# Ending instruction-prefetch hints before the second phase, and a refitted instruction order, in a memory-augmented transformer block

## The chip, the cores and the metric

The kernel runs on one core of a Trainium2 chip, as one program. The metric is the device time of one execution in microseconds, as a median of runs. A core has five engines that run their own instruction streams side by side: TensorE (PE, matmuls; its weight loads are listed as PEld), VectorE (DVE), ScalarE (ACT), GpSimd (POOL) and SyncE (SP, which issues the DMAs here). They wait for each other through semaphores.

## What is computed

A sequence of 2048 tokens (512 wide, bf16) goes through a layer norm and an attention layer with 32 heads of 128, in 64 segments of 32 tokens. Each segment attends to itself and to 8 memory tokens, and the memory of the next segment is the attention's output for those 8 tokens. So the 64 segments are a chain. Then comes an MLP (512 to 1792 to 512, gelu) over all tokens, with residuals.

```python
for s in range(n_seg):                                  # 64
    xs = x[:, s * seg_len:(s + 1) * seg_len, :].copy()
    h = jnp.concatenate([mem, xs], axis=1)              # 8 + 32 rows
    q = jnp.einsum('btd,dhe->bhte', h, Wq)
    k = jnp.einsum('btd,dhe->bhte', h, Wk)
    v = jnp.einsum('btd,dhe->bhte', h, Wv)
    scores = jnp.einsum('bhqe,bhke->bhqk', q, k) * scale
    scores = jnp.where(mask[None, None], scores, -1000000000.0)
    p = _softmax(scores, axis=-1)
    o = jnp.einsum('bhqk,bhke->bhqe', p, v)
    o = jnp.einsum('bhte,hed->btd', o, Wo)
    mem = o[:, :M, :].copy()                            # 8 rows go on to s + 1
    outs.append(o[:, M:, :])
...
h = x + _A_ref(_layernorm(x, axis=-1), ...)
h2 = h + _B_ref(_layernorm(h, axis=-1), ...)            # gelu(y @ w1 + b1) @ w2 + b2
```

## The kernel before

**Two phases.** The first phase walks through the 64 segments. Four segments make a block of 128 tokens; a segment's place in its block (0 to 3) is called first to fourth segment here. The second phase is the MLP, in four groups of 512 tokens.

**A segment on PE.** 24 of its 32 tokens and the 8 memory tokens are one group of 32 rows (A); the remaining 8 tokens of four segments are packed into one group of 32 rows per block (B). The parts of a segment have names:

- K0, K1, Q0, Q1, V0, V1: the projections of A, half the heads each. One is four passes over the inner dimension (L680; L446 where the weights of the pass before are kept in place and not loaded again), each of four matmuls side by side.
- SC0, SC1: scores of the memory rows and of B (L821); PV0, PV1: their products with the values (L851, L855).
- SA: scores of the A rows (L880); PVA: their product with the values (L906), done in the segment after.
- WO: the output projection in eight units (L943). Its memory rows, turned by DVE (TT, L955) and added (hT, L949), are what K0 of the next segment waits for.
- F0, F1: projections of the next block's B rows, in the first three segments of a block; FB: the output projection of the B rows, in the fourth.
- TR: a layer norm or a residual step that brings no PE work in most segments.

Between them the other engines empty PSUM and do the softmax. On ACT: kqP0 to kqP3 (projections out of PSUM), EC (exp of SC), VS (values), OT (outputs), prefills of PSUM with masks ("ps"). On DVE: KA and QT (32x32 transposes of keys and queries), nmc, rsc, PC, PTC (softmax of SC), nma, SA, sma, rsa, PTA (softmax of SA), TT and hT, opA and opB, xr, st and st2 with ag and ag2 (layer norm statistics). On POOL: ZC (copies of queries that SC needs), PA (part of SA's softmax).

**What sets the order.** PE's order is written out by hand in ORDER, one row for each of a block's four segments, with slices of parts ("K0", 0, 3 is the first three passes of K0). BANKS gives the PSUM bank of each part, BACK says which projections run through the inner dimension backwards (so that weights can be kept). The other engines' orders come from a list scheduler, Sched.schedule, that works with assumed durations: each operation has a rank (the longest way to the end) plus a bonus by its kind, from the table BONUS, and is placed on its engine in the earliest gap. Where an operation may run on several engines (for example ZC on ACT, DVE or POOL), the earliest end wins, and DVE is charged LEAN on top. DMAs are issued by SP, in the order of their planned starts.

**Instruction pages and hints.** Sched.far cuts PE's stream so that a branch lies near the end of each stretch of 256 instructions. Cut k has a branch that is never taken (zero < 0) to the place two cuts further on, and a prefetch hint for it that stands just after the cut before. The branch's fall-through is the next instruction, so the program's order isn't changed by it. The hint names a target three pages ahead of the page that it stands in. At the last two cuts there is a plain branch to the next instruction and no hint. In the kernel before there are 173 cuts.

Of the kernel before, what the change touches and what calls it, by code (L numbers as in the profile page):

```python
# [19 lines left out]
OVERLAP = {"act": 0.1, "dve": 0.077, "pool": -0.06, "sp": 0.0}  # L20
DMA_SEMS = 100
STIR = 12
LINE_N, LINE_AT, LINE_HINT, LINE_LAST, LINE_FIRST, LINE_Q, LINE_W = 256, 192, 172, 228, 80, 24, 0.005
HALVES = ("kqP", "KA", "ZCm", "QA", "VS", "nmc", "EC", "rsc", "PC", "PTC", "OTm", "KB", "QTB", "VSB", "QT")
BONUS = {"EC1": -9.35, "KA1": -9.25, "KB0": 1.83, "KB1": 1.99, "OTB": -7.01, "OTm1": 2.33, "PA": 4.46, "PC0": -2.44, "PC1": -9.37,
         "PTA": -0.66, "PTC0": -17.49, "QT0": 16.34, "QT1": -16.16, "QTB0": -4.17, "SA": -3.48, "TT": 3.09, "VBD": 15.9, "VS0": -6.6,
         "VS1": -4.52, "VSB1": -1.12, "ZCb": -3.7, "ZCm0": 4.94, "ZCm1": 0.49, "ag": 40, "ag2": -18.63, "hTx": 5.11, "hd": 4.63,
         "kqP0": -1.58, "kqP1": -0.51, "kqP2": 0.34, "kqP3": 16.53, "kqP4": 8.98, "kqP5": -11.25, "nma": 2.14, "nmc0": 10.03, "nmc1": 7.47,
         "opA": -22.54, "opB": -40, "ps": -10.18, "rs": 9.93, "rs2": -4.63, "rsa": 3.13, "rsc0": 3.57, "rsc1": -3.63, "sma": -5.97,
         "st": 4.73, "st2": -7.47, "vd": -9.08, "xT": 3.91, "xn": 4.97, "xn4": 0.15, "xr": -40}  # L30
LEAN = 7.140

ORDER = (
          (("K0", 0, 4), ("Q0", 0, 4), ("Q1", 0, 4), ("K1", 0, 4), ("SC0", 0, 1), ("V0", 0, 1), ("TR", 0, 1), ("V0", 1, 4), ("V1", 0, 2),
           ("SC1", 0, 1), ("F0", 0, 2), ("V1", 2, 3), ("PVA", 0, 1), ("PV0", 0, 1), ("V1", 3, 4), ("F0", 2, 4), ("WO", 0, 2),
           ("PV1", 0, 1), ("WO", 2, 8), ("F1", 0, 4), ("SA", 0, 1)),
          (("K0", 0, 3), ("Q0", 0, 1), ("K0", 3, 4), ("Q0", 1, 4), ("Q1", 0, 4), ("K1", 0, 4), ("SC0", 0, 1), ("V0", 0, 1), ("TR", 0, 1),
           ("V0", 1, 4), ("V1", 0, 2), ("SC1", 0, 1), ("F0", 0, 1), ("V1", 2, 3), ("F0", 1, 2), ("PVA", 0, 1), ("PV0", 0, 1), ("V1", 3, 4),  # L40
           ("F0", 2, 4), ("WO", 0, 2), ("PV1", 0, 1), ("WO", 2, 8), ("F1", 0, 4), ("SA", 0, 1)),
          (("K0", 0, 4), ("Q0", 0, 4), ("Q1", 0, 4), ("K1", 0, 4), ("SC0", 0, 1), ("V0", 0, 1), ("TR", 0, 1), ("V0", 1, 4), ("V1", 0, 2),
           ("SC1", 0, 1), ("F0", 0, 1), ("V1", 2, 3), ("F0", 1, 2), ("PVA", 0, 1), ("PV0", 0, 1), ("V1", 3, 4), ("F0", 2, 4), ("WO", 0, 2),
           ("PV1", 0, 1), ("WO", 2, 8), ("F1", 0, 4), ("SA", 0, 1)),
          (("K0", 0, 3), ("Q0", 0, 1), ("K0", 3, 4), ("Q0", 1, 4), ("Q1", 0, 4), ("K1", 0, 4), ("SC0", 0, 1), ("PVA", 0, 1), ("V0", 0, 1),
           ("TR", 0, 1), ("V0", 1, 4), ("SC1", 0, 1), ("FB", 0, 1), ("V1", 0, 3), ("PV0", 0, 1), ("V1", 3, 4), ("FB", 1, 4), ("WO", 0, 2),
           ("PV1", 0, 1), ("WO", 2, 8), ("FB", 4, 8), ("SA", 0, 1)),
)
BANKS = (
    dict(Q0=5, Q1=7, K0=4, K1=5, V0=7, V1=5, SC0=6, SC1=4, F0=6, F1=5, FB=5, SA=7, WO=4),  # L50
    dict(Q0=5, Q1=7, K0=4, K1=5, V0=7, V1=5, SC0=6, SC1=4, F0=6, F1=5, FB=5, SA=7, WO=4),
    dict(Q0=5, Q1=7, K0=6, K1=5, V0=7, V1=5, SC0=6, SC1=4, F0=6, F1=5, FB=6, SA=7, WO=4),
    dict(Q0=5, Q1=7, K0=4, K1=5, V0=7, V1=5, SC0=6, SC1=4, F0=5, F1=7, FB=6, SA=7, WO=4),
)
BACK = (("Q0", "Q1", "V1"), ("Q0", "Q1", "V0", "F0", "F1"), ("Q1", "K0", "V0", "F0", "F1"), ("Q0", "V1"))
BANK0 = dict(K0=7, K1=5, Q0=6, Q1=7, V0=4, V1=5, SC0=4, SC1=6, F0=6, F1=4, FB=6, SA=4, WO=5)
START = (("B", "V", 0, (6, 7)), "V0", "V1", ("B", "K", 0, (4, 6)), "K0", "K1", ("B", "K", 1, (4, 6)), ("B", "V", 1, (7, 5)),
         ("B", "Q", 0, (4, None)), "Q0", ("B", "Q", 0, (None, 5)), "Q1", "Z", "SC0", "SC1", ("B", "Q", 1, (5, 7)), "PV0", "PV1", "SA", "WO")
# [24 lines left out]
class Sched:  # L83
# [89 lines left out]
    def schedule(self):  # L173
# [25 lines left out]
        def push(o):  # L199
            heapq.heappush(heap, (-o.rank - BONUS.get(o.kind, 0.0), o.gidx, o))  # L200
        for o in self.rec:
# [13 lines left out]
        for o in order:  # L215
# [13 lines left out]
            for eng, (fn, dur) in (o.alts or {o.eng: (o.fn, o.dur)}).items():  # L229
                L, ST = lines[eng], starts[eng]  # L230
                i = bisect.bisect_right(ST, t)
                while True:
# [7 lines left out]
                    i += 1  # L240
                cost = s + dur + (LEAN if eng == "dve" and o.alts else 0.0)
                if best is None or cost < best[0]:
# [77 lines left out]
    def far(self, nc, e, zero):  # L320

        ops = self.streams["pe"]
        early, per, m = None, [], 0
        for o in ops:
            per += [o.dur / o.ni] * o.ni
        n, lines, cuts, cand = 0, -2, [], []
        for i, o in enumerate(ops):
            line, at = divmod(n - LINE_AT, LINE_N)
            if early is None and line == -1 and at >= LINE_FIRST:
                early = i  # L330
                n += 1
                line, at = divmod(n - LINE_AT, LINE_N)
            if cand and (line > cand[0][0] or at >= LINE_LAST):
                cuts.append(max(cand, key=lambda c: c[1:])[-1])
                lines = cand[0][0]
                cand = []
                n += 2
                line, at = divmod(n - LINE_AT, LINE_N)
            if line > lines and at >= LINE_HINT:
                assert at < 240  # L340
                cand.append((line, min(sum(per[max(0, m - LINE_Q):m]), 0.4) + min(sum(per[m:m + LINE_Q]), 0.3) + at * LINE_W, i))
            m += o.ni
            n += o.ni + (len(o.waits) >= 2)
        cuts += [c[-1] for c in cand[-1:]]
        home, mark, k = nc.cur_bb.parent, None, 0
        for i, o in enumerate(ops):
            if i == early:
                mark = e.mark_branch_hint_location()
            if k < len(cuts) and cuts[k] == i:
                if k + 2 < len(cuts):  # L350
                    b = e.br_lt(zero, 0, on_true="line%d" % (k + 2), on_false="line%d" % k)
                    if mark is not None:
                        b.branch_hint(mark)
                    nc.switch_bb("line%d" % k, parent=home)
                    mark = e.mark_branch_hint_location()
                else:
                    e.br("line%d" % k)
                    nc.switch_bb("line%d" % k, parent=home)
                k += 1
            yield o  # L360
# [103 lines left out]
def build_kernel(nc, A_x, A_mem0, A_Wq, A_Wk, A_Wv, A_Wo, B_w1, B_b1, B_w2, B_b2, out):  # L464
# [3 lines left out]
    with st:  # L468
# [461 lines left out]
        def wo_units(lhs, reads, bank, idle=None):  # L930

            for q in range(8):
                if idle and q == 4:
                    stir(*idle)

                def f(e, q=q):
                    for k in (2 * q, 2 * q + 1):
                        for a in range(2):

                            h = (k // 8) * 16 + 8 * a + k % 8  # L940
                            for b in range(2):
                                j = 2 * a + b
                                ins = e.matmul(ps[bank][32 * j:32 * j + 32, 0:256], lhs(slot(h)), wo_cols(h, b), start=(k == 0), stop=(k == 15),  # L943
                                               tile_position=(0, 32 * j), skip_group_check=True)
                    return ins
                S.op("pe", f, reads=[("WO", 2 * (q // 4) + g) for g in range(2)] + reads(q // 4), writes=[("ps", bank)], dur=0.2185, mode=MC, ni=16)
# [4 lines left out]
        def wo(s, bank, mem=True, xrows=True):  # L951
            par = s % 2
            wo_units(lambda sl: OT[:, par, sl, :], lambda r: [("OTm", par, r), ("OTx", par)], bank, None if s else (STIR, 7))
            tt = TT[:, par]
# [142 lines left out]
        def backs(name):  # L1097
            return now[0] > 0 and name in BACK[now[0] % 4]

# [214 lines left out]
```

## Time and profile before

| | |
|---|---|
| time before, median of 20 runs | 831.86 us (828.42 to 835.56) |
| the profiled execution, its own time | 831.87 us |
| its span, first to last instruction | 830.0 us |
| granted TensorE clock in it | 0.992 of full speed |
| PE matmuls, 22170 records | busy 783.8 us, 94% of the span |
| ACT | busy 571.1 us, 69% |
| DVE | busy 527.8 us, 64% |
| POOL | busy 159.6 us, 19% |
| instruction queue of PE | 172 packets, 2.82 MB |

The span falls into four stretches: up to 52.8 us the loads of the four large weights set the pace; from there to about 84 us the first block, in which there is no F and no FB; from 84 to about 664 us fourteen blocks alike; from 664 to 733 us the last block and the hand-over to the second phase, in which W1 and W2 are loaded over the keys' weights; from 733 us the second phase, on PE throughout.

In a timeline, each line gives the start in us, the duration, the engine, the line of the kernel, the operation and its tiles, the number of instructions merged, and in brackets the idle time before the first of them with what ended it. "issue" is idle time in which the engine waited for nothing that the profile shows.

### The profile page before, as it was taken

Reading aid. Unit: us, or ns where it says so; the run is one execution under the profiler, and the core shown is the slowest. Engines: PE = TensorE matmul, PEld = TensorE weight load, DVE = VectorE, ACT = ScalarE, POOL = GpSimd, SP = SyncE. Lnnn points to the kernel's source line nnn. Section 1 sums busy time; section 2 is a strip of 40 time slices with the busy share of each in tenths; the row PEclk is TensorE's granted clock in tenths of the full one; section 3 lists DMA queues with packets and bytes.
Section 4 is the critical chain, followed back from the end, with each engine's and each line's share of the span. In section 5 each row is a group of like instructions: output and inputs, shape, how many; then the busy total and the mean of one; then the engine's idle time right before and its main releaser. Section 6 shows DMA issues by size and latency. Waiting matters only on the chain.

```text
span 830.0 us, 48268 instructions
## 1 busy us (share of the span) xinstructions
PE 783.8 (94%) x22170; PEld 435.0 (52%) x21429; DVE 527.8 (64%) x1651; ACT 571.1 (69%) x1579; POOL 159.6 (19%) x390
## 2 busy tenths in 40 slices
PE   1888999999999999999999999999999989799998
PEld 0334555555555555555555555555555544454443
DVE  3157676878787878777877777777777776422111
ACT  1456787778777878787878787878787867434442
POOL 3223111212121212121212121111111111052200
PEclk9989999999999999999999999999999999899999
DMA  8980001111111111111111111010000110601000
GB/s 329 369 225 16 4 17 29 30 30 30 30 30 29 30 29 30 30 30 29 30 30 31 28 30 31 25 28 24 23 25 22 49 30 4 230 28 37 25 26 25
DMA packets 50407, 44.13 MB, mean 53 GB/s; under 512 B 17940, under 2 KB 46492, under 8 KB 50204
## 3 DMA queue, kind: packets, MB, share of 16 engines
q1 hardware_dynamic: 49756, 40.53, 16.5%
q8 instruction: 172, 2.82, 1.4%
q0 software_dynamic: 448, 0.53, 0.3%
q14 instruction: 31, 0.25, 0.1%
HBM read 28.98 MB, written 8.39 MB: 45 GB/s over the span
## 4 chain that ended last, share of the span: by engine, by line
PE 86%; DMA 6%; DVE 4%; ACT 2%; issue 1%; POOL 0%; SPq 0%
PE ps L680 41%; PE ps L943 18%; PE ps L1203 6%; PE quad L1210 6%; PE ps L446 4%; PE quad L851 3%; DMA WO<-in_A_Wo_dram 2%; PE ps L821 2%; PE quad L906 2%; DMA WV<-in_A_Wv_dram 2%; PE ps L880 2%; DMA WQ<-in_A_Wq_dram 1%; DMA WK<-in_A_Wk_dram 1%; ACT EC L833 1%; PE quad L855 1%
## 5 line engine op out<-in xcount | busy, mean ns | idle before, releaser
L680 PE MATMUL ps<-WV,hT 128*32 128x512 bf16 x1860 | 145.4, 383 | 0.0
L943 PE MATMUL ps<-WO,OT 128*32 128x256 bf16 x4224 | 139.5, 274 | 2.5 <-DMA WO<-in_A_Wo_dram 1.0
L680 PE MATMUL ps<-WK,hT 128*32 128x512 bf16 x1732 | 115.9, 380 | 6.5 <-DVE hT L949 6.2
L680 PE MATMUL ps<-WQ,hT 128*32 128x512 bf16 x1796 | 120.2, 381 | 0.0
L694 ACT CAST kqP<-ps 128x512 bf16<-128x512 f32 x160 | 92.7, 579 | 37.6 <-PE ps L680 28.3
L943 PEld LDWEIGHTS ps<-WO,OT 128*32 128x32 bf16 x4224 | 100.5, 96 | 26.6 <-ACT OT L694 5.0
L895 POOL TENSOR_TENSOR PA<-SA,rsa 128x256 bf16<-128x256 f32 x64 | 39.5, 617 | 353.1 <-DVE rsa L894 353.1
L695 ACT ACTIVATE kqP<-ps 128x512 bf16<-128x512 f32 x160 | 95.7, 598 | 13.1 <-PE ps L680 7.0
L694 ACT CAST OT<-quad 128x128 bf16<-128x128 f32 (+1 forms) x192 | 85.0, 443 | 24.5 <-PE quad L855 15.0
L722 DVE STREAM_TRANSPOSE KALL<-kqP 128x256 uint32<-128x256 uint32 x160 | 67.9, 424 | 29.4 <-ACT kqP L694 25.4
L680 PEld LDWEIGHTS ps<-WQ,hT 128*32 128x32 bf16 x1796 | 48.3, 97 | 69.7 <-issue 28.1
L833 ACT ACTIVATE EC<-ps,nmc 128x64 f32<-128x64 f32 x256 | 77.7, 308 | 6.2 <-DVE nmc L829 6.1
L694 ACT CAST VS<-ps 128x512 bf16<-128x512 f32 x128 | 75.1, 586 | 6.9 <-PE ps L680 5.3
L1206 ACT ACTIVATE WQ<-ps,b1t 128x512 bf16<-128x512 f32 x56 | 38.5, 687 | 59.5 <-PE ps L1203 59.1
L955 DVE STREAM_TRANSPOSE TT<-ps 128x256 f32<-128x256 f32 x66 | 29.7, 450 | 69.0 <-PE ps L943 69.0
L892 ACT ACTIVATE SA<-SA 128x256 f32<-128x256 f32 x64 | 26.7, 417 | 62.3 <-DVE SA L891 62.2
L680 PEld LDWEIGHTS ps<-WK,hT 128*32 128x32 bf16 x1732 | 38.2, 95 | 54.8 <-issue 16.3
L680 PEld LDWEIGHTS ps<-WV,hT 128*32 128x32 bf16 x1860 | 48.6, 97 | 34.9 <-issue 16.4
L722 DVE STREAM_TRANSPOSE QT<-kqP 128x256 uint32<-128x256 uint32 x128 | 55.8, 439 | 5.8 <-ACT kqP L695 2.6
L1210 PE MATMUL quad<-WK,WQ 128*128 128x512 bf16 x217 | 53.7, 379 | 0.9 <-DVE xr L996 0.5
L1255 DVE TENSOR_TENSOR WV<-quad,WV 128x512 bf16<-128x512 f32 x16 | 11.1, 692 | 65.8 <-PE quad L1210 65.7
L821 PEld LDWEIGHTS ps<-KALL,ZC 128*32 128x32 bf16 x2048 | 31.6, 96 | 39.4 <-issue 17.5
(116 smaller groups left out, 1324.2 us busy)
## 6 DMA issues: line engine op xcount, KB each, us to landing
WV<-in_A_Wv_dram SPq DMA_DIRECT2D x4, 1024.0 KB, 9.3
WK<-in_A_Wk_dram SPq DMA_DIRECT2D x4, 1024.0 KB, 8.5
WQ<-in_A_Wq_dram SPq DMA_DIRECT2D x4, 1024.0 KB
WO<-in_A_Wo_dram SPq DMA_DIRECT2D x4, 1024.0 KB, 10.5
v_last<-VSB SPq DMA_DIRECT2D x60, 64.0 KB, 2.1
VBD<-v_last SPq DMA_DIRECT2D x60, 64.0 KB
xr<-in_A_x_dram SPq DMA_DIRECT2D x16, 128.0 KB, 3.4
h_mid<-xr SPq DMA_DIRECT2D x16, 128.0 KB, 1.8
```

The lines of the kernel that those rows point to most:

```text
L446: return e.add_instruction(mybir.InstMatmult(name="I-%d" % (4000000 + _kept[0]), engine=mybir.EngineType.PE, start_tensor_calc=start, stop ...
L680: ins = e.matmul(o, l, m, start=start, stop=stop, tile_position=(0, 32 * j), skip_group_check=True)
L694: return {"act": (lambda e: e.copy(out, src), t_act(n, ps_)), "dve": (lambda e: e.tensor_copy(out, src), 0.165 + 1.0e-3 * n * fast)}
L695: return {"act": (lambda e: e.mul(out, src, scale_), t_act(n, ps_)), "dve": (lambda e: e.tensor_scalar(out, src, scale_, None, ALU.mult), ...
L722: S.op("dve", lambda e: e.transpose(dst.bitcast(U32), kqP[:, i, :].bitcast(U32)), reads=[("kqP", i)], writes=[key], dur=0.435)
L821: ins = e.matmul(ps[bank][32 * j:32 * j + 32, 64 * sl:64 * sl + 64], ZC[:, par, h, :], rhs, start=False, stop=(i == 3), tile_position=(0, ...
L833: ins = e.activation(EC[:, r, sl, :], ps[bank][:, 64 * sl:64 * sl + 64], ACTF.Exp, bias=nmc[:, r, sl:sl + 1], accum_out=smc[:, r, sl:sl + 1])
L895: pa = lambda e: e.tensor_tensor(PA[:], SA[:], bc(rsa), ALU.mult)
L943: ins = e.matmul(ps[bank][32 * j:32 * j + 32, 0:256], lhs(slot(h)), wo_cols(h, b), start=(k == 0), stop=(k == 15), tile_position=(0, 32 * ...
L1203: ins = e.matmul(ps[bank][:, 0:SBT], W1[:, cc, fc * P:(fc + 1) * P], hnT_of(k, cc // 2)[:, cc % 2, :], start=(cc == 0), stop=(cc == DC - 1))
L1206: S.op("act", lambda e: e.activation(gT[:, fc, :], ps[bank][:, 0:SBT], ACTF.Gelu_apprx_tanh, bias=b1t[:, fc:fc + 1], scale=1.0), reads=[(" ...
L1210: S.op("pe", lambda e: e.matmul(quad[:, t, :], gT[:, fc, t * P:(t + 1) * P], W2[:, fc, :], start=(fc == 0), stop=(fc == FC - 1)), reads=[" ...
```

## The change

The change has two parts. In Sched.far, the list of cuts ends two cuts after the last cut that is planned to lie less than LINE_SLOW (4 us) before the next. What lies behind has no branches and no hints. This leaves 168 cuts of 173: five branches and five hints are gone, and the last hint stands in page 163 and asks for page 166 (pages of 256 instructions, numbered as in the first kernel's stream, where the second phase begins in page 166).

The rest are new tables: ORDER, BANKS, BACK, BONUS and LEAN. No function other than far is touched.

```diff
+LINE_SLOW = 4.0
...
-LEAN = 7.140
+LEAN = 1.487
...
 ORDER = (
-          (("K0", 0, 4), ("Q0", 0, 4), ("Q1", 0, 4), ("K1", 0, 4), ("SC0", 0, 1), ("V0", 0, 1), ("TR", 0, 1), ("V0", 1, 4), ("V1", 0, 2),
-           ("SC1", 0, 1), ("F0", 0, 2), ("V1", 2, 3), ("PVA", 0, 1), ("PV0", 0, 1), ("V1", 3, 4), ("F0", 2, 4), ("WO", 0, 2),
-           ("PV1", 0, 1), ("WO", 2, 8), ("F1", 0, 4), ("SA", 0, 1)),
-          (("K0", 0, 3), ("Q0", 0, 1), ("K0", 3, 4), ("Q0", 1, 4), ("Q1", 0, 4), ("K1", 0, 4), ("SC0", 0, 1), ("V0", 0, 1), ("TR", 0, 1),
...
-          (("K0", 0, 3), ("Q0", 0, 1), ("K0", 3, 4), ("Q0", 1, 4), ("Q1", 0, 4), ("K1", 0, 4), ("SC0", 0, 1), ("PVA", 0, 1), ("V0", 0, 1),
-           ("TR", 0, 1), ("V0", 1, 4), ("SC1", 0, 1), ("FB", 0, 1), ("V1", 0, 3), ("PV0", 0, 1), ("V1", 3, 4), ("FB", 1, 4), ("WO", 0, 2),
-           ("PV1", 0, 1), ("WO", 2, 8), ("FB", 4, 8), ("SA", 0, 1)),
+          (("K0", 0, 1), ("Q0", 0, 4), ("K0", 1, 4), ("Q1", 0, 4), ("K1", 0, 4), ("SC0", 0, 1), ("V0", 0, 4), ("V1", 0, 2), ("SC1", 0, 1),
+           ("V1", 2, 3), ("F0", 0, 2), ("PVA", 0, 1), ("PV0", 0, 1), ("V1", 3, 4), ("F0", 2, 4), ("WO", 0, 2), ("PV1", 0, 1), ("WO", 2, 8),
+           ("TR", 0, 1), ("F1", 0, 4), ("SA", 0, 1)),
+          (("K0", 0, 4), ("Q0", 0, 4), ("Q1", 0, 4), ("K1", 0, 4), ("SC0", 0, 1), ("V0", 0, 4), ("V1", 0, 2), ("SC1", 0, 1), ("F0", 0, 2),
...
+          (("K0", 0, 3), ("Q0", 0, 1), ("K0", 3, 4), ("Q0", 1, 4), ("Q1", 0, 4), ("K1", 0, 4), ("SC0", 0, 1), ("V0", 0, 4), ("V1", 0, 2),
+           ("SC1", 0, 1), ("FB", 0, 2), ("V1", 2, 3), ("PVA", 0, 1), ("PV0", 0, 1), ("V1", 3, 4), ("FB", 2, 4), ("WO", 0, 2),
+           ("PV1", 0, 1), ("WO", 2, 8), ("FB", 4, 6), ("TR", 0, 1), ("FB", 6, 8), ("SA", 0, 1)),
 )
...
-BACK = (("Q0", "Q1", "V1"), ("Q0", "Q1", "V0", "F0", "F1"), ("Q1", "K0", "V0", "F0", "F1"), ("Q0", "V1"))
+BACK = (("Q0", "K0", "K1", "V1"), ("Q0", "K0", "K1", "V0"), ("Q0", "K0", "V0", "V1", "F0", "F1"), ("K1", "V0"))
...
         cuts += [c[-1] for c in cand[-1:]]
+        last = max(k for k in range(len(cuts) - 1) if ops[cuts[k + 1]].start - ops[cuts[k]].start < LINE_SLOW)
+        cuts = cuts[:last + 3]
```

BONUS has new values throughout. What the new tables do to the engines' orders is seen in the built programs' instruction lists (kinds of operations, without times):

| where | before | after |
|---|---|---|
| PE, fourth segment | SC0, PVA, V0, SC1, FB, V1, PV0 | SC0, V0, V1, SC1, FB, V1, PVA, PV0 |
| PE, second segment | K0 (3 passes), Q0 (1), K0 (1), Q0 (3) | K0 (4), Q0 (4) |
| PE, first segment | K0 (4), Q0 (4) | K0 (1), Q0 (4), K0 (3) |
| ACT, first segments from 8 on | SA kqP0 kqP2 ps ps kqP3 kqP1 EC0 VS0 | SA kqP2 kqP0 ps ZCm0 kqP3 ps kqP1 EC0 VS0 |
| DVE, first segments from 8 on | rsa KA0 QT0 PTA QT1 | rsa QT0 KA0 PTA QT1 |
| ACT, other segments from 5 on | EC0 VS0 ps EC1 | EC0 VS0 EC1 ps |
| DVE, segment 1 | PTA TT hT st ag st ag KA0 QT0 xn QT1 | PTA st TT ag hT st ag xn st KA0 ag xn QT0 QT1 |
| DVE, segment 3 | KA0 xn PTA QT0 QT1 | KA0 QT0 PTA QT1 |
| DVE, segment 61 | nma SA TT sma rsa hT opA PTA xr st2 KA0 ag2 QT0 QT1 | TT hT nma SA opA sma rsa KA0 xr QT0 PTA QT1 |
| DVE, segments 62, 63 | KA0 PTA QT0 QT1 | KA0 QT0 PTA QT1 |
| SP, after the fourth WO load | vd vd vd vd xr xr xr xr xr | xr vd vd vd vd xr xr xr xr |

In the other segments of the middle, DVE's order is the same in both. POOL's order differs by the 15 ZC copies that go to ACT. 156 groups of four matmuls keep their weights instead of 189.

## Prediction

> **What bounds the kernel now.** I read the page's busy table and slices first, then the stretches by stage, then who TensorE (PE) waited for, then the timelines of the places where it stood still.
>
> The page:
> ```profile
> PE 783.8 (94%) x22170; PEld 435.0 (52%) x21429; DVE 527.8 (64%) x1651; ACT 571.1 (69%) x1579; POOL 159.6 (19%) x390
> ```
> Stretches (PE, PEld, DVE, ACT, POOL busy, clock, DMA share, GB/s): one period of four segments in the middle, then three segments of the last block and the hand-over to the second phase.
> ```profile
> 622.40:663.80 41.40, 41.33 (x1356) 23.81 (x1300) 30.55 (x98) 32.35 (x96) 7.19 (x18) 1.00 0.13 35
> ...
> 676.60:689.60 13.00, 9.70 (x320) 5.34 (x300) 8.64 (x26) 7.52 (x22) 2.35 (x6) 1.00 0.21 25
> 689.60:700.20 10.60, 9.73 (x309) 5.12 (x296) 6.51 (x22) 8.58 (x24) 1.20 (x3) 1.00 0.02 5
> ...
> 711.50:733.30 21.80, 15.87 (x299) 9.53 (x296) 10.29 (x30) 7.53 (x11) 1.50 (x3) 0.84 0.39 137
> ```
> In the middle PE is busy 41.33 of 41.40 us while ACT and DVE are near 77%: only a shorter PE order helps there. The last block and the hand-over have PE holes. Up to 52.8 us the chain of waits is the weight loads; from 733 us PE is full again.
>
> PE's waits (total us, times, longest):
> ```profile
> PE ps L680 <- DVE hT L949: 6.2, 5, 3.0
> PE quad L906 <- issue: 4.7, 1, 4.7
> ```
> PE's timeline at the second, and the DMA of that hole:
> ```profile
> 716.22 0.29 PE L906 MATMUL quad<-PTA,VS 32*128 32x24 bf16 x19
> 721.23 0.27 PE L906 MATMUL quad<-PTA,VS 32*128 32x24 bf16 x13 [4.71 <-issue]
> ```
> ```profile
> q8 instruction: 1, 0.02, 1.2%
> ```
> The hole is inside one operation of 32 matmuls, after the 19th; no semaphore can end there. Counted from the start of PE's stream it is a boundary of 256 instructions, and one 16 KB packet of the instruction queue moves inside the hole: a missed instruction page, 4.71 us.
>
> DVE's timeline before the 3.0 us wait:
> ```profile
> 677.13 0.42 DVE L890 TENSOR_REDUCE nma<-ps 128x8 f32<-128x256 f32 x1 [1.70 <-PE ps L880]
> 677.59 0.42 DVE L891 TENSOR_TENSOR SA<-ps,nma 128x256 f32<-128x256 f32 x1
> 677.93 0.44 DVE L955 STREAM_TRANSPOSE TT<-ps 128x256 f32<-128x256 f32 x1
> ...
> 679.18 0.72 DVE L949 TENSOR_TENSOR hT<-TT 64x32 bf16<-64x32 f32 x2
> ```
> PE ended WO at 676.58. DVE idled, ran two softmax steps first, then TT, and hT after two more; PE restarted at 679.95.
>
> PE inside a fourth segment (first three lines) and in a second one (last two):
> ```profile
> 577.52 0.31 PE L821 MATMUL ps<-KALL,ZC 128*32 128x64 bf16 x16
> 577.76 0.37 PE L906 MATMUL quad<-PTA,VS 32*128 32x24 bf16 x32
> 578.06 1.05 PE L680 MATMUL ps<-WV,hT 128*32 128x512 bf16 x16
> ```
> ```profile
> 590.24 0.37 PE L906 MATMUL quad<-PTA,VS 32*128 32x24 bf16 x32
> 590.66 0.27 PE L851 MATMUL quad<-PTC,VS 32*128 32x16 bf16 x16
> ```
> PVA alone (577.76) pays its own way in and out of the row-tiled mode.
>
> [...] an operation before such a change takes 0.12 us more (0.34 instead of 0.22 start to start, passes before PVA). [...] the trace has the missed page while W1 and W2 (3.6 MB) load.
>
> **The change, part by part.**
>
> 1. *Fourth segment: PVA moves next to PV0.* Medians of start-to-start steps over the middle. Before: scores to PVA 0.24, PVA to pass 0.30, pass to PV0 0.325, together 0.86. After: scores to pass 0.12, pass to PVA 0.34, PVA to PV0 0.215, together 0.68. That is 0.18 in 15 segments, 2.7 us, all on PE. What may be late next is PV0's PTC0: in the other segments, which already have this order, PV0 waits 0.04 to 0.08 on average; in 15 segments 0.6. Net -2.1 (bounds -2.7 and -0.5).
>
> 2. *Second segment: K0 no longer split by Q0.* It takes the order of the first segment before. Mean lengths are 10.35 and 10.26 with the same PE floor of 10.18; 14 segments times 0.09 is 1.2. I take half, -0.6 (0 to -1.2).
>
> 3. *First segment: Q0 inside K0; ACT takes kqP2, kqP0, one prefill, ZCm0, kqP3.* Fifteen ZC copies leave POOL for ACT. In the trace ACT starts one cast 0.5 after another and a prefill 0.2 after. Before: kqP0 503.11, kqP2 503.62, two prefills 504.11, kqP3 504.50. After: one prefill goes behind kqP3 and ZCm0 takes its 0.2; kqP3 still starts at 504.50, when Q1 is ready. Cost 0; if that slot is gone, V0 (same bank as Q1) waits 0.2 in 14 segments, +2.8. Elsewhere EC1 goes ahead of the SA prefill: 0.1 earlier for a PV1 that isn't waiting. Banks and the order of weights: 33 more groups of four matmuls load their weights, which costs nothing as long as a pass with kept weights and one without both step 0.22, as they do now.
>
> 4. *Segment 61: TT and hT first on DVE.* TT can start 0.23 after WO's end (as at 511.18 after 510.95), 676.81; with TT 0.45 and hT 0.39 PE restarts at 677.74 instead of 679.95: -2.2. Given back: xr (0.38) now stands before QT and st2 (0.66) before rsc1. I charge 0.5. Net -1.7 (-2.2 to -1.0). xr waits for the transpose issued at 675.45; with 3.1 us to land that is 678.6, before its turn near 680.
>
> 5. *Segments 62 and 63, and 2 to 4: QT0 before PTA on DVE.* PTA waits for POOL's PA (0.42 at 692.88) with QT behind it, and scores start at 694.10, 0.53 after the passes end. After, QT0 follows KA0 at once, and ZC fits. 0.5 each, -1.0. In the first block scores come 0.70, 0.84 and 0.78 after the last pass's start, against 0.24 to 0.27 normally: -0.35, -0.57, -0.3. Segment 1 loses: three BN steps and an xn (0.66, 0.16, 0.37) go before QT0, about +0.5; st before TT costs little if x's second block lands with the last WO (52.8). Together -1.7 (-2.6 to -0.3).
>
> 6. *The hints.* Before, each page is asked for three pages ahead; [...] (in the trace's DMA records the instruction packets after the page entries at 704.8 and 711.3 start 3.7 and 3.8 us later; in the middle it is about 1). After, the last hint brings page 166, before W1 starts; five hints go, and page 167 must come by ordinary prefetch when 166 is entered. That this exists is shown by the last page, never hinted: its packet moves at 796.6, 2.3 us after PE's sequencer enters the page before, and nothing stands still at 826.4. By the new order page 166 is entered at what was 709.6 and 167 needed at what was 713.9: 4.3 us, against about 5 from request to use under this load (4.7 in the hole). A stall of 0.9 remains, so -3.8 (bounds -4.7 and 0). From page 168 on a page lasts 9 to 28 us, which covers 5.
>
> Sum of parts 1 to 6: -2.1 - 0.6 + 0 - 1.7 - 1.7 - 3.8 = -9.9. The profiled execution took 831.87 us (span 830.0), 0.01 above the median of the 20 runs, so **822.0 us**.
>
> **Rivals.**
>
> *A. Page 167 is late all the same.* For: only 4.3 us, under load; no ordinary fetch under load is in the trace. Then part 6 gives nothing: 831.9 - 6.1 = 825.8.
>
> *B. The order's gain is eaten by new waits.* For: ACT and DVE have half a us of slack before PV0 and V0; part 3's slot is filled to 0. Against: outside the edges the engines' orders hardly differ. Then parts 1 and 2 end at 0, parts 4 and 5 at half, the hints stay: 831.9 - 3.8 - 1.7 = 826.4; if the hints fail too, 830.2.
>
> *C, slower. Pages without a hint come only on demand.* The place is every boundary from 167 to 172. The price is 4.7 for 167, as now, and for the five after it about 3.4 each (1.0 from hint to packet, 1.0 transfer, 1.4 from the packet's end at 719.8 to the restart at 721.2): 17. It decides once more than two such boundaries stand fully open (6.1 / 3.4). 831.9 - 6.1 + 17 = 842.8; part may hide in PE's queue, since the sequencer runs 2.6 us ahead there. Against: the last page. The same price would apply to pages lost in the middle, whose boundaries all move.
>
> **How the numbers follow.** Forecast 0.62 (own range 818.5 to 825), A 0.18, B 0.10, C 0.08, and 0.02 for nothing at all. The range 817.5 to 829 takes the forecast, A and most of B, with the bounds of parts 1 to 6. A measurement of this kernel tells 0.2% (1.7 us) from no change: faster than that are the forecast, A and most of B, 0.87; within it a rest of B and nothing, 0.04; slower is C and what is left, 0.09.
>
> **What would show it.** In the profile after: PVA directly before PV0 in fourth segments and a period near 41.1; K0 of segment 61 about 1.2 after WO, not 3.4; scores of 62, 63 without 0.8 before them; the 4.7 issue wait gone or under 2. Wrong if PE shows issue waits at several boundaries of the second phase, or in the middle, or if V0 waits for kqP in first segments.

## The result, and the profile after

| | before | after |
|---|---|---|
| time, median | 832.04 us (826.63 to 835.56, 47 runs) | 819.61 us (819.13 to 821.28, 7 runs) |
| ratio after/before, 95% interval | | 0.9859 (0.9841 to 0.9877) |
| span of the profiled execution, clock | 830.0 us, 0.992 | 817.8 us, 0.998 |

The page after, each engine's share:
```profile
PE 776.8 (95%) x22170; PEld 435.6 (53%) x21561; DVE 527.1 (64%) x1651; ACT 568.3 (69%) x1594; POOL 155.7 (19%) x375
```
PE is busy 7.0 us less with the same 22170 recorded matmuls. No matmul was removed. The mean clock rose from 0.992 to 0.998, which is worth up to 5 us (an estimate: 0.006 of 820 us); what the rest of the 7.0 is was not taken apart. The other 5.2 of the 12.2 us are holes that are gone.

The stretches after, that answer to those of before (us; PE, PEld, DVE, ACT, POOL busy; clock; DMA share; GB/s): a middle period, segment 61, and the hand-over.
```profile
611.60:652.70 41.10, 41.04 (x1348) 23.97 (x1304) 30.39 (x99) 32.19 (x95) 6.93 (x17) 1.00 0.13 36
...
672.60:683.90 11.30, 9.84 (x319) 5.38 (x298) 8.12 (x26) 7.61 (x23) 2.40 (x6) 1.00 0.11 28
...
704.60:721.60 17.00, 13.68 (x299) 8.68 (x292) 10.64 (x32) 7.79 (x11) 1.51 (x3) 1.00 0.54 191
```
Segment 61 takes 11.30 instead of 13.00 us. The hand-over runs the same 299 matmuls in 17.00 us; the line of before, 21.80, ends half a microsecond short of the first W2 matmul, and up to that matmul it is 22.28. Its clock is 1.00, not 0.84, and PE's busy time fell from 15.87 to 13.68: the clock column of the former line stands for 2.2 us beside its hole of 4.7. The middle period shown here is 0.3 us shorter than the one before, but that lies in the choice of the period: the mean period over segments 8 to 59 fell from 41.44 to 41.32 us.

PE's waits after:
```profile
PE ps L683 <- DVE hT L952: 4.0, 5, 1.0
...
PE ps L946 <- issue: 1.6, 1, 1.6
```
The longest wait for hT is 1.0 (3.0 before), and the late page is late by 1.6 (4.7 before).

Where the time went, from the start of each segment's SA on PE to the next, in both traces; "first" to "fourth" are means over the 13 segments of that place in segments 8 to 59:

| stretch | before | after | difference, all its segments |
|---|---|---|---|
| up to SA of segment 1 | 64.10 | 63.31 | -0.79 |
| segments 2, 3, 4 | 10.63, 11.02, 11.71 | 10.27, 10.17, 11.36 | -1.56 |
| segments 5 to 7 | 31.15 | 30.98 | -0.17 |
| first | 10.281 | 10.258 | -0.30 |
| second | 10.355 | 10.425 | +0.91 |
| third | 10.284 | 10.349 | +0.84 |
| fourth | 10.516 | 10.293 | -2.90 |
| segment 60 | 9.29 | 9.29 | 0 |
| segment 61 | 12.97 | 11.25 | -1.72 |
| segment 62 | 10.61 | 10.21 | -0.40 |
| segment 63 | 11.35 | 10.48 | -0.87 |
| hand-over: SA of 63 to the first W2 matmul | 22.27 | 17.07 | -5.20 |
| second phase | 96.18 | 96.19 | 0 |

Together -12.15, the difference of the two spans (12.2).

The hand-over of the kernel before, PE's timeline behind the hole that the prediction showed:
```profile
721.43 1.03 PE L1203 MATMUL ps<-QTB,WK 128*128 128x512 bf16 x2
...
732.02 0.59 PE L1203 MATMUL ps<-QTB,WK 128*128 128x512 bf16 x2
```
and of the kernel after:
```profile
706.43 0.84 PE L946 MATMUL ps<-WO,OT 128*32 128x256 bf16 x24 [0.51 <-ACT SA L895]
708.89 1.27 PE L946 MATMUL ps<-WO,OT 128*32 128x256 bf16 x40 [1.63 <-issue]
...
711.37 0.61 PE L1206 MATMUL ps<-QTB,WK 128*128 128x512 bf16 x2
```
The same pairs of matmuls last 1.03 right after the hole of 4.71 us and 0.59 ten us later; after the hole of 1.63 they last 0.61 at once. About five pairs start 0.85 apart instead of 0.43: the hole cost 2.1 us more behind its own end.

### The profile page after: what moved, and what is told of

It is laid out like the page before. It is cut to its first block, busy times and chain, and to the rows that moved or that the text cites. A ratio compares the mean times of both kernels' runs of the same rounds, so it can differ in the third digit from the quotient of the medians.

```text
span 817.8 us, 48387 instructions
## 1 busy us (share of the span) xinstructions
PE 776.8 (95%) x22170; PEld 435.6 (53%) x21561; DVE 527.1 (64%) x1651; ACT 568.3 (69%) x1594; POOL 155.7 (19%) x375
## 4 chain that ended last, share of the span: by engine, by line
PE 88%; DMA 6%; DVE 2%; ACT 2%; issue 1%; SPq 0%; POOL 0%
PE ps L683 44%; PE ps L946 19%; PE quad L1213 6%; PE ps L1206 6%; PE ps L449 4%; PE quad L854 3%; DMA WO<-in_A_Wo_dram 2%; PE quad L909 2%; PE ps L824 2%; DMA WV<-in_A_Wv_dram 2%; PE ps L883 2%; DMA WQ<-in_A_Wq_dram 1%; ACT EC L836 1%; DMA WK<-in_A_Wk_dram 1%; PE quad L858 1%
## 5 line engine op out<-in xcount | busy, mean ns | idle before, releaser
L683 PE MATMUL ps<-WV,hT 128*32 128x512 bf16 x1860 | 142.5, 381 | 0.0
L683 PE MATMUL ps<-WK,hT 128*32 128x512 bf16 x1860 | 128.3, 381 | 4.2 <-DVE hT L952 4.0
L683 PEld LDWEIGHTS ps<-WK,hT 128*32 128x32 bf16 x1860 | 43.0, 95 | 56.3 <-issue 17.4
```

The costliest lines, as they stand in the source:

```text
L683: ins = e.matmul(o, l, m, start=start, stop=stop, tile_position=(0, 32 * j), skip_group_check=True)
```

## The experiments

Twelve kernels, in five groups. Times are medians; "segments" are measured in each kernel's own profile as in the table above. The time up to segment 1 varies by up to 1.6 us between these profiles (62.97 to 64.61), with the first loads and with the length of a stretch there in which the clock record shows 0.5 (3.4 to 13.7 us), also where nothing before it was changed, so small effects are read from the segments. The mean of one place differs by up to 0.03 us between profiles with the same order in it; less than that is not read.

**The hints.**

*The new order with all hints.*
```diff
-        last = max(k for k in range(len(cuts) - 1) if ops[cuts[k + 1]].start - ops[cuts[k]].start < LINE_SLOW)
-        cuts = cuts[:last + 3]
```


> The kernel after, but with hints and branches up to the end of the program (173 cuts, not 168); all orders are those of after. Theory L [...]: in the new order page 166 has landed at 696.7, before W1 starts to load, [...] the 1.6 us issue wait goes, and the time is about 818. Theory E [...]: the hole of 4.7 us comes back, with TensorE at half clock after it for another 2.1 us: about 824.8. Rival N (the hints' end did nothing, the order did it all): 819.6, with the 1.6 us wait as in after.

820.5 us (820.31 to 823.49), ratio 0.9882 (0.985 to 0.9914). Page 167, which is late by 1.63 us in the changed kernel, is in time here, and page 168 is late by 2.63. So theory L was right about page 167 and wrong about the total, which lies nearest to rival N's. The hand-over takes 18.17 us: the new order with all hints brings it from 22.27 to 18.17, and the end of the hints from there to 17.07. With the new order it is worth 1.1 us, and the single runs of the two kernels overlap.

*The former order with the hints' end.*
```diff
+LINE_SLOW = 4.0
...
+        last = max(k for k in range(len(cuts) - 1) if ops[cuts[k + 1]].start - ops[cuts[k]].start < LINE_SLOW)
+        cuts = cuts[:last + 3]
```


> The kernel before with the hints' end alone (168 cuts); all orders are those of before. Theory (the change's hand-over gain is the hints' doing): the issue wait of 4.7 us falls to 0 to 1.6 and the half clock after it goes (2.1 us), so 5.2 faster than before, about 826.8. Rival N (the order did it): about 832, hole as before.

826.16 us (824.19 to 827.54), ratio 0.9937 (0.9916 to 0.9957). Its PE timeline at the place of the former hole:
```profile
716.42 0.31 PE L909 MATMUL quad<-PTA,VS 32*128 32x24 bf16 x22
717.43 0.23 PE L909 MATMUL quad<-PTA,VS 32*128 32x24 bf16 x10 [0.70 <-issue]
717.59 0.60 PE L1206 MATMUL ps<-QTB,WK 128*128 128x512 bf16 x2
```
The same boundary, without a hint: 0.70 late instead of 4.71, and PE goes on at full speed (0.60 a pair). The hand-over is 16.13 instead of 22.27; the segments before it are as they were within 0.05 us. So with the former order the end of the hints alone is worth 6.1 us in the profile (5.2 by the ratio), as the theory said, and pages from 168 on come without a hint and in time.

*The changed kernel with no hints behind the 84th.*
```diff
-        cuts = cuts[:last + 3]
+        cuts = cuts[:84]
```


> The kernel after with hints only up to the middle of the program (84 cuts), so that some 88 pages of about 4 us in the second half come by ordinary prefetch. Theory O (an ordinary prefetch is asked for when the page before is entered): [...] most pages are in time; 820 to 830, holes of up to 1 us at the shortest pages. Rival D (without a hint a page comes on demand): about 3.4 us at each of some 80 boundaries in the first phase, 1050 to 1100 us.

845.57 us (one run), span 843.8, 26.0 above the changed kernel: +19.3 in segments 8 to 59, +5.8 in segment 63. PE's waits:
```profile
PE ps L946 <- issue: 8.1, 8, 3.9
```
Neither range held. 26 us over 88 pages is 0.3 each on average (24 pages are visibly late), not the 3.4 that the prediction charged for a page on demand: the other 64, without a hint too, are not. The 22 pages that are late before W1 and W2 are loaded start 3.0 to 5.0 us, 3.9 in the median, after the page before was entered; a page in the middle lasts some 3.9 us. When a page without a hint is asked for, no record shows. In the middle the hints earn their place; at the hand-over it depends on the page, as the next kernel shows.

*The changed kernel with one hint more.*
```diff
-        cuts = cuts[:last + 3]
+        cuts = cuts[:last + 4]
```


> The changed kernel with one hint more (for the page that holds the start of the second W2 pass's neighbourhood, the page that the changed kernel's profile has late by 1.63 us); no instruction of an engine changes its order. Theory L (a hint given as early as this one, before W1's block is loaded, still lands in time): the late-page hole before L946/L1203 goes from 1.63 to under 0.3 us, the hand-over from 17.07 to about 15.5, total about 818.0. Rival M [...]: the hole stays at 1.6 or grows to 2.6 as with all hints kept, total 819.5 to 820.6. Both leave the stages before segment 63 as they were (within 0.3 us in sum).

817.97 us (817.64 to 818.22), ratio 0.985 (0.9791 to 0.9908); span 816.5. Its PE timeline where the changed kernel had 1.63:
```profile
706.43 1.93 PE L946 MATMUL ps<-WO,OT 128*32 128x256 bf16 x64 [0.51 <-ACT SA L895]
```
WO runs through its 64 matmuls, as theory L said. By the DMA records the packet behind the entry of page 166 moves 1.02 us after it instead of 3.77. The hand-over is 15.76. For this order the hints ended one too early.

**The fourth segments.**

*The former kernel with PVA alone moved next to PV0.*
```diff
-... ("SC0", 0, 1), ("PVA", 0, 1), ("V0", 0, 1), ... ("V1", 0, 3), ("PV0", 0, 1),
+... ("SC0", 0, 1), ("V0", 0, 1), ... ("V1", 0, 3), ("PVA", 0, 1), ("PV0", 0, 1),
```


> The kernel before with PVA next to PV0 in the fourth segments and nothing else in ORDER; apart from two places in segments 3 and 63 every engine's order is as before. Theory: 0.2 us in each of 14 to 15 segments, 2.5 to 3.0 us faster, about 829.3, with fourth segments of 10.3 us, not 10.5. Rival: PV0 then waits for its softmax and the time stays at 832.

833.63 us (828.75 to 839.27), ratio 1.0029 (1.0009 to 1.005): slower, which neither expectation had. Fourth segments take 10.706 instead of 10.516. PE in one of them:
```profile
495.39 1.05 PE L680 MATMUL ps<-WV,hT 128*32 128x512 bf16 x16
496.56 0.31 PE L821 MATMUL ps<-KALL,ZC 128*32 128x64 bf16 x16
```
Four V0 passes start 0.216 apart, so SC1 could start at 496.25; it starts at 496.56. On average it comes 0.53 after the pass before it, not 0.22, and in all 13 places the trace has DVE's transpose of the keys (KA) as what released it. PVA and the two longer steps at it (0.24 and 0.30 in the kernel before) had filled that time; with them gone, SC1 waits longer than these steps had cost.

*The former kernel with the whole new fourth row* (SC1 also goes behind two V1 passes, FB and TR move).
```diff
-... ("PVA", 0, 1), ("V0", 0, 1), ("TR", 0, 1), ("V0", 1, 4), ("SC1", 0, 1), ("FB", 0, 1), ("V1", 0, 3), ("PV0", 0, 1), ...
+... ("V0", 0, 4), ("V1", 0, 2), ("SC1", 0, 1), ("FB", 0, 2), ("V1", 2, 3), ("PVA", 0, 1), ("PV0", 0, 1), ...
```


> The kernel before with the whole fourth row of ORDER of the kernel after (PVA next to PV0 and, with it, SC1 two V1 passes later and FB, TR moved), nothing else. Theory W (the gain of the fourth segments needs SC1 moved back as well, since with PVA alone moved SC1 waited 0.53 for KA1 and ZCm1): fourth segments go from 10.516 to about 10.29, 13 times .22 = 2.9 less, total about 829.1 against 832.0. Rival X (the gain comes from the other rows or from the vector engines' orders, as with PVA alone moved, 10.706): fourth segments stay at 10.5 or above, total 832 or more.

829.19 us (827.26 to 830.93), ratio 0.9967 (0.9951 to 0.9983). SC1 starts 0.216 after the pass before it. Fourth segments are 10.403, halfway between 10.516 and 10.293: neither expectation. The total lies at the first one's value by luck, since the late pages moved too (167 by 0.73 us, 168 by 3.37) and the hand-over got 1.06 shorter. The missing 0.11 shows in two steps: PV0 comes 0.280 after PVA (0.216 in the changed kernel), and SC0 0.268 after K1's last pass (0.239).

The first of these is no wait for another engine. From PVA's start to PV0's it takes 0.21 to 0.27 us or 0.39 to 0.51, and never anything between. The changed kernel in a fourth segment:
```profile
504.27 0.37 PE L909 MATMUL quad<-PTA,VS 32*128 32x24 bf16 x32
504.50 0.28 PE L854 MATMUL quad<-PTC,VS 32*128 32x16 bf16 x16
```
This is a short step; the pair at 590.24 and 590.66 that the prediction shows is a long one. There a branch of Sched.far falls between the two: by the trace's records PE's sequencer runs the branch at 590.33, the hint at 590.47 and a semaphore wait at 590.55. Over all 14 profiles, from 90 to 660 us, 177 such pairs have a branch in the half microsecond before PV0, and all 177 are long (0.42 to 0.51); of the 546 others four are. And the kernel without hints behind the 84th, in the same order as the changed one, has no such branches behind 365 us and none of its 27 pairs from 365 to 660 us long, where the changed kernel has 9 of 29. So a branch between PVA and PV0 costs 0.22 us (0.42 to 0.51 against 0.21 to 0.27). In the fourth segments from 8 to 59 one falls there four times of 13 in this kernel and never in the changed one, which makes 0.07 of the 0.11. Where it falls depends on the number of instructions before it, so also on which weights are kept; that the changed kernel's fourth segments go free is luck of the count. What lengthens SC0's step no run separates.

**The second and third segments, which got longer.**

*The changed kernel with K0 and Q0 of the second row split as before.*
```diff
-          (("K0", 0, 4), ("Q0", 0, 4), ("Q1", 0, 4), ("K1", 0, 4), ("SC0", 0, 1), ...
+          (("K0", 0, 3), ("Q0", 0, 1), ("K0", 3, 4), ("Q0", 1, 4), ("Q1", 0, 4), ("K1", 0, 4), ("SC0", 0, 1), ...
```


> The changed kernel with K0/Q0 of the second segments split again as in the kernel before (K0 passes 0 to 2, Q0 pass 0, K0 pass 3, the rest of Q0); only segments 1 and 61 change otherwise. Theory S (the unsplit order made the second segments' K1 wait longer, 0.288 instead of 0.239 a step): mean of the second segments goes from 10.425 back to about 10.355, 13 times .07 = 0.9 less; total about 818.7, less what segments 1 and 61 change (segment 61 may lose up to 0.5). Rival T (the wait comes from elsewhere, such as the evictions on ACT that were moved in all rows): the second segments stay within .02 of 10.425 and the total at 819.6.

818.73 us (818.54 to 820.02), ratio 0.9864 (0.9805 to 0.9923). Second segments 10.373 instead of 10.425; K1's first pass comes 0.233 after Q1 instead of 0.288. In the trace it is released by ACT's cast (kqP), which empties the bank that K1 shares with Q0; 9 of 13 K1s come late without the split, one with it. Segment 61, which was to lose, gains 0.38. So theory S holds here, at the size of 0.05. It doesn't hold everywhere: with BACK's third row as before, the second segments take 10.370 without the split (next experiment) and 10.373 with it (the last kernel of this section), and K1 comes late 6 and 7 times. By the medians alone the split isn't told apart from the changed kernel.

*The changed kernel with the third row of BACK as before.*
```diff
-BACK = (..., ("Q0", "K0", "V0", "V1", "F0", "F1"), ...)
+BACK = (..., ("Q1", "K0", "V0", "F0", "F1"), ...)
```


> The changed kernel with the third row of the reversed passes (BACK) as in the kernel before; each engine issues the same operations in the same order of kinds, only the order of the passes in a block, and with it which weights are kept from block to block, is the former one. Theory K (reloading weights ahead of the scores block is what made the third segments slower): their mean goes from 10.349 to about 10.285, 13 times .065 = 0.85 less; total about 818.8. Rival N (reloading is hidden, the loss is a wait for evictions): third segments stay within .02 of 10.349, total 819.6. As pages shift by a few loads, the hole at the hand-over may move by up to 1 us either way; the segment means decide.

818.96 us (818.05 to 820.12), ratio 0.9865 (0.9806 to 0.9925). Third segments 10.334, not 10.285: reloaded weights are not the reason, and the theory falls. Second segments came to 10.370 and fourth ones to 10.358, whose own rows weren't touched: with other weights kept, the branches fall between PVA and PV0 once instead of six times in the second segments, and four times instead of never in the fourth. The late page was 1.1 us late at another place. Of the 0.065 by which the third segments got longer, 0.03 is such branches (five instead of three in 13), and 0.03 is SC0, which comes 0.268 after K1's last pass instead of 0.236 in every one of them. What holds SC0 up stays open.

**DVE's order at the edges.**

*The former kernel with TT and hT of segment 60 first* (a priority for these operations and for the operation that frees TT's buffer).
```diff
+            if s == 60:
+                S.rec[-1].kind = "T60"
```


> The kernel before, where DVE runs TT and hT of segment 60 ahead of the memory rows' softmax steps (nma, SA) at the start of segment 61, as the changed kernel does; nothing else on PE, ACT or before that point changes (in segment 61 xr, PTA, QT0 follow in this order, two rs2 on POOL go behind the ZC copies). Theory (part 4 of the prediction): K0's wait of 3.0 to 3.4 in segment 61 falls to about 1.2, segment 61 from 12.97 to about 11.3 to 11.5 (xr before PTA and QT0 gives some back), total about 830.4 against 832.0. Rival (the memory rows' softmax, now later by 0.9, holds up PVA or the scores instead): segment 61 stays above 12.3 and the total within 0.7 of before.

830.06 us (825.3 to 833.72), ratio 0.9974 (0.9956 to 0.9991). DVE at the start of segment 61:
```profile
675.91 0.45 DVE L955 STREAM_TRANSPOSE TT<-ps 128x256 f32<-128x256 f32 x1 [1.39 <-PE ps L943]
676.40 0.39 DVE L949 TENSOR_TENSOR hT<-TT 64x32 bf16<-64x32 f32 x2
676.82 0.42 DVE L890 TENSOR_REDUCE nma<-ps 128x8 f32<-128x256 f32 x1
```
TT is now ahead of nma. Segment 61 takes 11.46 instead of 12.97, and the longest wait for hT is 1.0. The theory holds, for the segment and for the total.

*The former kernel with QT0 ahead of PTA in segments 2, 3, 4, 62 and 63.*
```diff
+LATE = {"PTA1": 0.35, "PTA2": 0.35, "PTA3": 0.35, "PTA61": 0.15, "PTA62": 0.25}
...
+            t += LATE.get(o.kind, 0.0)
```


> The kernel before, where DVE runs QT0 ahead of PTA in segments 2, 3, 4, 62 and 63, by hand-set delays of PTA in the order's model; the orders of PE are unchanged. Theory (part 5): the scores of these five segments no longer wait behind PTA; segment 2 from 10.63 to 10.3, 3 from 11.02 to 10.3, 4 from 11.71 to 11.4, 62 from 10.61 to 10.2, 63 from 11.35 to 10.9, together about -2.2 us, total about 829.8. Rival (PTA comes late for PVA, or the scores waited for K's transposes anyway): the five segments lose less than 0.8 together, total 831.2 or more; the last segment is the likeliest to give it back, since PVA stands early in the former fourth row.

825.08 us (824.34 to 827.1), ratio 0.9915 (0.9898 to 0.9933): far more than expected. The five segments: 10.27, 10.46, 11.21, 10.06, 10.69, together -2.63; the theory holds. But the hand-over fell too, from 22.27 to 17.53, though all 173 hints are there. Its PE timeline:
```profile
713.05 0.37 PE L910 MATMUL quad<-PTA,VS 32*128 32x24 bf16 x32
...
722.13 1.16 PE L947 MATMUL ps<-WO,OTB 128*32 128x256 bf16 x34 [1.99 <-issue]
723.23 0.61 PE L1207 MATMUL ps<-QTB,WK 128*128 128x512 bf16 x2
```
The 32 matmuls of PVA, in which the former kernel lost 4.71, run through; page 168 is late by 1.99, and no half speed follows. From the DMA records of four kernels with all hints and the former tail:

| kernel | page 164 entered | W1's first packet | instruction packet after the entry | page 167 late |
|---|---|---|---|---|
| before | 704.80 | 705.45 | 3.7 | 4.71 |
| TT first | 702.40 | 703.05 | 3.7 | 4.7 |
| PVA alone moved | 706.37 | 707.02 | 4.1 | 4.45 |
| QT0 first | 701.76 | 702.94 | 1.1 | none |

With 0.65 us between the entry and W1's first packet, the instruction packet comes only during the load and page 167 is late; with 1.18 us it moves just ahead of the load. Half a microsecond of order goes with the 4.7; by what mechanism, the records don't show. Four profiles agree in this; no run moved the start of the load alone.

**Combinations of what helped.**


> The changed kernel with one hint more and with K0/Q0 of the second segments split as before. If the two gains add (1.6 from the hint, 0.9 from the split): 817.1, no issue wait at the hand-over. If they interact (the page shift by the split makes another page late): 818 or more.

One hint more and the split (the two diffs above): 817.53 us (817.37 to 817.9), ratio 0.9819 (0.9806 to 0.9833), span 815.9, between the two expectations. The hand-over is 15.80, second segments 10.383, segment 61 10.86. This is the fastest version, 2.1 us under the changed kernel's median, and the two intervals against the kernel before (0.9806 to 0.9833, 0.9841 to 0.9877) don't touch. Against one hint more alone (817.97) it isn't told apart.

> As the kernel with the two, and the third row of BACK as before. If the middle's 0.5 from it holds and the extra hint still covers page 167: 816.6. If the hint falls on another block by the shifted pages and comes too late: a hole of 1 us or more returns at the hand-over and the total is 817.5 or more.

With BACK's third row as well: 818.67 us (818.43 to 818.72), ratio 0.9832 (0.9818 to 0.9845). Segments 8 to 59 take 536.63 instead of 536.83, less apart than two profiles of one order can be, and the hand-over stays (15.85). In the profile segment 1 ends 1.16 later: between 45 and 53 us the clock granted was 0.61, not 0.91. But that can't be why the median is 1.1 higher: the mean clock of the profiled run was 0.992, the four others had 0.998 and took 818.43 to 818.70 all the same. So 817.5 or more came true, without the hole that was to be its reason, and the reason stays open.

## Why the prediction was right or wrong

The forecast was 822.0; 819.6 is 2.4 lower, within its range. That it came so near is in part luck: steps 2 and 3 missed by 2.0 us to the slow side, steps 1, 5 and 6 by 4.1 to the fast side. Per step:

| step | predicted | in the traces |
|---|---|---|
| 1, fourth segments | -2.1 | -2.90 in the middle |
| 2, second segments | -0.6 | +0.91 |
| 3, first segments, ACT, weights | 0 | -0.30, and +0.84 in the third segments |
| 4, segment 61 | -1.7 | -1.72; alone -1.51 |
| 5, QT0 before PTA | -1.7 | -0.79, -1.56 and -1.27; alone -2.63 |
| 6, the hints | -3.8 | -5.20 |

1. The size came near, the mechanism only in part. The longer steps at PVA are real: the steps named in the sum fell by 0.20, where it has 0.18. But "what may be late next is PV0's PTC0" named the wrong wait. SC1 was next, and with PVA alone moved it turned the gain into a loss of 0.19 a segment. The 0.04 to 0.08 that was charged to PTC0 is about the mean price of the branches between PVA and PV0 (three of 13 at 0.22). The changed kernel gains because its row moves SC1 as well; half of the gain comes from outside this row, most of that from branches that fall elsewhere.

2. Wrong in sign. The step that begins "It takes the order of the first segment before" compared mean lengths of two places and took the difference for the split's price (over segments 8 to 59 the first place has 10.28, not 10.26). The split was paying for itself: without it K1 waits 0.055 longer for its bank. The other 0.02 of the second segments' 0.07 is within what the branches cost, which fall between PVA and PV0 six times of 13 instead of three.

3. The slot on ACT held, and V0 waits no longer than before. The third segments' loss was not on the list. That it comes from reloaded weights was tried and refuted; half of it is branches, the other half SC0's step, whose cause is open.

4. Right, in place and size: K0 starts 1.16 after WO's end instead of 3.37, which is 2.2 us, and 0.5 of it is given back, as charged.

5. Right in mechanism. Alone it gives 0.36 to 0.66 a segment where the sum had 0.3 to 0.57, with the largest excess in segments 4 (0.50 for 0.3) and 63 (0.66 for 0.5); I had taken only each score's wait over a normal step. What else it spares there was not separated. In the changed kernel the rest of segment 63 (0.87 against 0.66 alone) fits PVA's move, 0.22 in a fourth segment. The 0.79 up to segment 1 lies within what the first loads and the clock there vary, so that the 0.5 that segment 1 was to lose can't be read: segment 1 itself is 1.00 longer, and the time up to it 1.78 shorter.

6. Right for the kernel that the prediction looked at: with the former order the end of the hints takes the hole away, and that alone gives 6.14. Incomplete for the change as a whole: the new order with all hints already has 4.10 of the 5.20, and the end of the hints adds 1.10 there. The two gains don't add up, and the sum gave all of it to the hints. Two terms were mis-sized. What remains of the hole is 1.63, more than the 0.9 of "A stall of 0.9 remains": from the entry of page 166 (702.57) to the restart (708.89) it took 6.3 us, not about 5. This alone would have given less than forecast. But the price of the hole was 4.71 plus 2.1 of half-speed work behind it. The stretch's clock of 0.84 stood in the lines that the prediction quoted, and its sum left it out.

Rival A (page 167 late anyway) is true in a small way: late by 1.63, and by 0.70 with the former order. Rival B has its loss in the second and third segments, 1.75 us, of which a part is branches and not waits, and it was outweighed. Rival C is refuted at its own place: in the changed kernel and in the former one with the hints' end no page from 168 on is late, and even half a kernel without hints costs 0.3 a page. The "1.0 from hint to packet" in its price is the figure that part 6 has from a page's entry to the packet; from a hint to the next packet it is 2.06 in the median (kernel before, hints from 100 to 650 us).

## What to carry to other kernels

A hole in TensorE's work has to be priced with the clock behind it: behind the one of 4.71 us, half-speed work cost 2.1 us more, behind the one of 1.63 none did. Read the PEclk column of its stretch before summing. An operation with long steps at it may be filling a wait (PVA alone moved: 0.19 us a segment slower); before moving it away, ask which operand the next operation on that engine gets last. Where a page of instructions is fetched beside a large load, its landing can go with half a microsecond of order (here page 167 was 4.45 to 4.71 us late with 0.65 us from a page's entry to the load, in time with 1.18): judge a change of the fetch with the order fixed, and judge a change of the order with the late pages counted apart. And when the mean of a step lies between two values that it takes, sort its cases before looking for a wait: here it was the kernel's own branches, and a mean had hidden them. The changed kernel still has 17 branches between PVA and PV0 from 90 to 660 us; at 0.22 each, moving them would be worth some 3.7 us (an estimate, not tried).

## What the runs showed of the hardware

The half speed. In all 14 profiles the clock record changes only at multiples of 3.41 us from one another; in the kernel before it shows 0.5 from 718.91 to 725.74, behind the hole of 4.71. In the tail, holes of 3.37, 3.86, 4.45 and 4.71 us are followed by half-speed work, holes of 1.63, 1.99, 2.63 and 3.0 are not. In the hole of 3.37, of the former kernel with the new fourth row:
```profile
722.31 3.37 PE L943 MATMUL ps<-WO,OT 128*32 128x256 bf16 x61 [3.37 <-issue]
725.62 0.60 PE L1203 MATMUL ps<-QTB,WK 128*128 128x512 bf16 x2
```
64 such matmuls last 1.93 elsewhere; these 61 last 3.37. In the first block half-speed work follows a hole of 2.31; the changed kernel:
```profile
38.48 1.05 PE L683 MATMUL ps<-WQ,hB 128*32 128x512 bf16 x8 [2.31 <-DMA WQ<-in_A_Wq_dram]
39.31 1.92 PE L683 MATMUL ps<-WQ,hT 128*32 128x512 bf16 x16
```
Sixteen of them last 1.04 in the middle. And in the changed kernel with BACK's third row as before, a hole of 2.53 at the same place is not followed by half speed. So the length of the hole alone doesn't tell the cases apart. How long PE was busy in a stretch of 3.41 us at the hole does for these seven (the stretches lie on the grid of each profile's clock record):

| kernel | stretch of 3.41 us | PE busy in it | clock behind it |
|---|---|---|---|
| new fourth row | 718.53 to 721.94 | 0.41 | half |
| half the hints | 723.42 to 726.83 | 0.86 | half |
| changed | 34.50 to 37.91 | 0.90 | half |
| before | 715.50 to 718.91 | 1.01 | half |
| before | 677.95 to 681.37 | 1.42 | full |
| BACK's third row | 37.07 to 40.49 | 1.48 | full |
| changed | 706.92 to 710.33 | 1.62 | full |

From 30 us on in the 14 profiles, all 16 stretches of that grid at full clock in which PE was busy up to 1.25 us were followed by half speed, 3 of 18 between 1.4 and 1.8, and none above. These are counts in this kernel's profiles; what sets the clock, no record shows.

The fetch. In the changed kernel with no hints behind the 84th, 88 pages of about 4 us come without a hint at 26 us together, 0.3 a page, 24 of them visibly late. Where a page is entered 0.65 us before the load of W1 and W2 (about 380 GB/s in the kernel before and in the changed one) or, in the changed kernel, during it, the next instruction packet moves 3.7 to 4.1 us after the entry; where it is entered 1.18 us before, after 1.1. With one hint more it moves after 1.02 at the entry for which the changed kernel has 3.77.

The branches. One that is never taken, with its hint, costs PE 0.22 us where it stands between PVA and PV0 (177 of 177 pairs). In WO's steps in the changed kernel's segments 8 to 59 that have one in the half microsecond before, it costs nothing: a step of four matmuls takes 0.109 us in the median with one (155 steps) and without one (573).
